# Block-sparse attention and a two-layer FFN on one core: K, Q and V loads moved out of the attention stages, turned heads spread over four PSUM spaces

## The chip, the core and the metric

The kernel runs on one NeuronCore of a Trainium2 chip. The metric is device time in microseconds of one execution; a figure for a kernel is the median of several executions. Engine names are those of the profile: PE multiplies matrices (PEld loads its weights), DVE is VectorE, ACT is ScalarE, POOL is GpSimd, SP is SyncE.

## The reference, cut to what matters

```python
def _attn_ref(q, k, v, sampled_blocks):          # q, k, v: 4 x 8 x 768 x 64
    block, n_blocks = 32, 24
    scores = scale * np.matmul(q, k.transpose(0, 1, 3, 2))
    mask = np.abs(blk_i - blk_j) <= 1
    mask = mask | (blk_i == 0) | (blk_j == 0) | (blk_i == n_blocks - 1) | (blk_j == n_blocks - 1)
    for qb in range(n_blocks):
        for kb in sampled_blocks[qb]:            # 3 sampled key blocks for each query block
            mask[qb * block:(qb + 1) * block, kb * block:(kb + 1) * block] = True
    attn = softmax(np.where(mask, scores, -1e9))
    return np.matmul(attn, v)

def _moe_ref(x, w_in, w_out):                    # x: 3072 x 512, w_in: 512 x 2048, w_out: 2048 x 512
    return (gelu_exact(x @ w_in) @ w_out)
```

The attention output of the four batches, heads side by side, is the x of the FFN.

## The kernel before

**Stages.** Each batch is cut into two halves of 384 tokens, which gives eight units, numbered 0 to 7. Units 0, 2, 4 and 6 are the first halves (they also do the first and last query blocks against all keys, the "dense" rounds), units 1, 3, 5 and 7 the second. The order is written out by hand and each engine runs its own list in that order: attention of unit 0, then for n = 0 to 7 the first FFN product of unit n (FFN1: eight calls of `ffn1_step`, each eight matmuls and one Gelu), and then the attention of unit n+1, with the matmuls of the second FFN product of unit n (FFN2) dealt out between its rounds by a quota. In the main loop (line 515) `fresh` says that unit n+1 begins a new batch: it holds for n = 1, 3 and 5. So a "first half" FFN1 is n = 0, 2, 4, 6 and a "second half" FFN1 is n = 1, 3, 5, 7.

**What a new batch needs.** K and Q of a batch arrive as four DMAs (`load_kq`, two of K into `kn`, two of Q into `qn`), V as eight, one per head (`load_v`, into the V columns of `kvs[b % 2]`). All are issued on POOL. For a new batch each pair of heads of K and Q is turned on PE (`turn_heads`, 16 transposes) into a PSUM tile and placed in SBUF (`place_heads`, K on DVE, Q on ACT); `prep` does the two with the one PSUM tile `psT`. Eight pairs (k0 to k3, q0 to q3) are done, one in each step s = 0 to 7 of the second-half FFN1. When K has been placed, DVE copies the key and value blocks that unit n+1 will read into `gb`: `gather_fixed` (five large copies) and `gather` (33 small copies of K and V columns together, at block numbers held in registers).

**When the loads go out.** `hold_loads(m)` is a copy of one element of `g` on POOL: POOL goes on only when the Gelu of FFN1 column block m is done, so the DMAs behind it wait for that. Four V loads of batch 1 are issued before the first attention; four more wait for step 0 of FFN1(0). K and Q of the next batch wait for the last step of the first-half FFN1 (`hold_loads(14)`), so they run in the attention that follows. The V loads of later batches go out four at a time at step 0 of each FFN1.

**PSUM.** `psA` has two buffers (scores, FFN1), `psV` one (attention output `av`), `psT` one (turned tiles), `psO` one (FFN2 output `op`). During FFN1 `psV` and `psO` hold nothing.

Of the kernel before, what the change touches and what calls it, by code (L numbers as in the profile page):

```python
# [10 lines left out]
BF16 = mybir.dt.bfloat16  # L11
I32 = mybir.dt.int32
AF = mybir.ActivationFunctionType
# [6 lines left out]
def kernel(  # L20
# [11 lines left out]
    P = 128  # L32
    B, H, S, D = q.shape
# [14 lines left out]
    PI = 8  # L48
    PP = S // PI
# [12 lines left out]
    psA = ctx.enter_context(tc.tile_pool(name="psA", bufs=2, space=PSUM))  # L62
    psV = ctx.enter_context(tc.tile_pool(name="psV", bufs=1, space=PSUM))
    psT = ctx.enter_context(tc.tile_pool(name="psT", bufs=1, space=PSUM))
    psO = ctx.enter_context(tc.tile_pool(name="psO", bufs=1, space=PSUM))
# [9 lines left out]
    k0 = qT1.rearrange("p (n c) -> p n c", c=KC)  # L75
# [21 lines left out]
    def keys(b):  # L97
        return k0 if b == 0 else kvs[b % 2][:, :, 0:KC]

    def load_kq(dst, src, b, hs):  # L100
        nc.gpsimd.dma_start(out=dst[0:PP, hs],
                            in_=src[b, hs].rearrange("h (p i) d -> p h (i d)", i=PI))

    def load_v(b, h):
        G, hh = divmod(h, 4)
        c0 = KC + V2 * G + VW * (hh % 2)
        nc.gpsimd.dma_start(out=kvs[b % 2][32 * hh:32 * hh + 32, 0:NB, c0:c0 + D],  # L107
                            in_=v[b, h].rearrange("(n p) d -> p n d", p=BL))
# [13 lines left out]
    def hold_loads(m):  # L122

        nc.gpsimd.tensor_copy(mark, g[0:1, m, 0:1])  # L124

    def ones(i):
        for hh in range(4):
            c0 = KC + VW * (hh % 2) + D
            nc.gpsimd.memset(kvs[i][32 * hh:32 * hh + 32, 0:NB, c0:c0 + V2 + 1:V2], 1.0)
# [46 lines left out]
    def block_numbers(js, engine):  # L176
        flat = vf.rearrange("o j r -> o (j r)")
        vals = []
        for c0 in range(js[0] * NR, (js[-1] + 1) * NR, 22):
            c1 = min(c0 + 22, (js[-1] + 1) * NR)  # L180
            _, got = nc.values_load_multi_w_load_instructions(
                flat[0:1, c0:c1], engines=[engine], min_val=0, max_val=NB,
                skip_runtime_bounds_check_because="block numbers are below the number of blocks")
            vals += got if isinstance(got, (tuple, list)) else [got]
        return {j: vals[NR * i:NR * i + NR] for i, j in enumerate(js)}

    def turn_heads(which, pr, pt):

        src = kn if which == "k" else qn
        for i in range(PI):  # L190
            for h2 in range(2):
                r = h2 ^ (pr // 2)
                nc.tensor.transpose(pt[64 * r:64 * r + 64, i, :],  # L193
                                    src[0:PP, 2 * pr + h2, i * D:(i + 1) * D],
                                    identity[0:PP, 0:PP])

    def place_heads(b, which, pr, pt, on_act):
        if which == "k":
            dst = keys(b)[:, 0:NB, BL * pr:BL * pr + BL].rearrange("q n (a i) -> q n a i", i=PI)
            seen = pt.rearrange("q i (n a) -> q n a i", n=NB)  # L200
            if on_act:
                nc.scalar.copy(dst, seen)
            else:
                nc.vector.tensor_copy(dst, seen)  # L204
        else:
            dst = qTs[b % 2][:, pr, :].rearrange("q (p i) -> q p i", i=PI)
            seen = pt.rearrange("q i p -> q p i")
            if on_act:
                nc.scalar.mul(dst, seen, 1.0 / 8.0)
            else:  # L210
                nc.vector.tensor_scalar_mul(dst, seen, 1.0 / 8.0)

    def prep(b, which, pr, on_act):
        pt = psT.tile([P, PI, PP], BF16, name="pt", tag="T")
        turn_heads(which, pr, pt)
        place_heads(b, which, pr, pt, on_act)

    def spare_key(b):
        kT = keys(b)
        nc.vector.tensor_copy(kT[:, NB, :], kT[:, 0, :])  # L220

    def gather_fixed(b, js, copy):

        kT, n, groups = keys(b), len(js), gb.rearrange("p (g x) -> p g x", x=GW)
        for lane in range(3):
            m = len(range(lane, n, 3))
            c0, j = BW + KC * lane, js[0] + lane - 1
            copy(groups[:, 0:m, c0:c0 + 3 * BW].rearrange("p g (w c) -> p g w c", c=BW)[:, :, :, 0:KC],
                 kT[:, j:j + 3 * m, :].rearrange("p (g w) c -> p g w c", w=3))
        copy(groups[:, :, 0:3 * KC].rearrange("p g (l c) -> p g l c", c=KC),  # L230
             kT[:, None, 0:1, :].to_broadcast([P, NG, 3, KC]))
        copy(groups[:, :, 4 * BW:GW].rearrange("p g (l x) -> p g l x", x=DW)[:, :, :, NR * BW:DW],
             kT[:, None, NB - 1:NB, :].to_broadcast([P, NG, 3, KC]))

    def gather(b, js, at, i0, c0=0, c1=BW, engine=None):

        src = k0 if (b, c1) == (0, KC) else kvs[b % 2][:, :, c0:c1]
        for i, j in enumerate(js, i0):
            for r in range(NR):
                (engine or nc.vector).tensor_copy(sampled(i, r)[:, None, c0:c1],  # L240
                                                  src[:, bass.ds(at[j][r], 1), :])
# [93 lines left out]
    def table(func):  # L335

        nc.scalar.activation(junk, zero[0:1, 0:1], func)  # L337
# [147 lines left out]
    DVE, POOL = mybir.EngineType.DVE, mybir.EngineType.Pool  # L485
    J0, J1 = units[0].js, units[1].js
    value_list()
    known = block_numbers(J0[:7], DVE)
    spaces = [psA.tile([P, 2, 1024], BF16, name="pk", tag="A") for _ in range(2)]
    spaces.append(psV.tile([P, 2, 1024], BF16, name="pq", tag="V"))  # L490
    spaces = [x[:, i, 0:S].rearrange("p (i c) -> p i c", i=PI) for x in spaces for i in range(2)]
    spaces.append(psT.tile([P, PI, PP], BF16, name="pt", tag="T"))
    spaces.append(psO.tile([P, PI, PP], BF16, name="pt", tag="op"))
    for i, (which, pr) in enumerate([(w, pr) for w in "kq" for pr in range(NPR)]):
        turn_heads(which, pr, spaces[i])
        place_heads(0, which, pr, spaces[i], True)
    spare_key(0)
    gather(0, J0[:7], known, 0, 0, KC)
    gather_fixed(0, J0, nc.vector.tensor_copy)
# [4 lines left out]
    others = block_numbers(J0[7:], POOL)  # L504
    gather(0, J0[7:], others, 7, 0, KC, nc.gpsimd)
    gather(0, J0[7:], others, 7, KC, BW, nc.gpsimd)
    ones(1)
    for h in range(4):
        load_v(1, h)
    attention(units[0], iter(()), [0] * 11, (0, 0), 7,  # L510
              {6: [lambda: gather(0, J0[:7], known, 0, KC, BW)]})
    nc.vector.tensor_copy(kvs[0][:, :, 0:KC], k0)
# [2 lines left out]
    for n, unit in enumerate(units):  # L515
        nxt = units[n + 1] if n + 1 < len(units) else None
        b = unit.b
        fresh = nxt is not None and nxt.b != b
        if nxt is not None and not fresh:
            gather_fixed(b, J1, nc.vector.tensor_copy)  # L520
            gather(b, J1[:6], known, 0)
            for i0, i1 in ((6, 9), (9, 11)):
                gather(b, J1[i0:i1], block_numbers(J1[i0:i1], DVE), i0)
        for s in range(KOUT // 2):
            ffn1_step(n, 2 * s)
            if s == 0:
                if not fresh and b + 1 < B:
                    hold_loads(0)
                    for h in range(4, H):
                        load_v(b + 1, h)  # L530
                if fresh and b + 2 < B:
                    hold_loads(0)
                    for h in range(4):
                        load_v(b + 2, h)
                if fresh:
                    others = block_numbers(J0[7:], DVE)
            if s == 7:
                if not fresh and b + 1 < B:
                    hold_loads(14)
                    for hs in HALVES:  # L540
                        load_kq(kn, k, b + 1, hs)
                    for hs in HALVES:
                        load_kq(qn, q, b + 1, hs)
                if nxt is not None:
                    table(AF.Exp)
            if fresh:
                prep(b + 1, "k" if s < 4 else "q", s % 4, s >= 4)
                if s == 3:
                    spare_key(b + 1)
                    gather_fixed(b + 1, J0, nc.vector.tensor_copy)  # L550
                    gather(b + 1, J0[:7], known, 0)
                    gather(b + 1, J0[7:], others, 7)
        filler = ffn2_pieces(n)
        if nxt is None:
            for _ in filler:
                pass
        elif fresh:
            attention(nxt, filler, [4] * 8 + [1, 1, 0], (3, 11))
        else:
            attention(nxt, filler, [6, 5, 5, 5, 5, 6, 2], (3, 11))  # L560
# [30 lines left out]
```

## Time and profile before

| what | value |
|---|---|
| median of 3 runs | 354.41 us (352.02 to 354.45) |
| the profiled execution | 352.95 us, of which the span from first to last instruction is 350.9 us |
| PE busy / weight loads | 277.8 us (79%) / 152.0 us (43%) |
| DVE busy | 220.3 us (63%) |
| ACT busy | 211.7 us (60%) |
| POOL busy | 51.4 us (15%) |
| mean granted clock of PE | 0.951 |
| DMA read and written | 27.26 MB and 6.29 MB |

The table is an average over stages with different limits. The stage is the thing to read: a period is the time from the first matmul of one FFN1 to the first matmul of the next, and holds one FFN1 and one attention. All four first-half periods run the same program on other data, and so do the three second-half periods.

### The profile page before, as it was taken

The page shows a single profiled execution, that of the slowest core. Times are in us where ns is not written, and L with a number is a line of the kernel's source. Part 1 is how long each engine was busy: PE and PEld are TensorE (multiplying, and loading weights), DVE is VectorE, ACT ScalarE, POOL GpSimd, SP SyncE. Part 2 cuts the span into 40 slices and gives each one's busy share as a digit, 9 for nine tenths or more (in the row PEclk, how much of TensorE's full clock was granted, in tenths as well). Part 3 has the DMA queues.
Part 4 walks back from the last instruction along what each step waited for, and adds up shares of the span by engine and source line. Part 5 has one row for each costly group of instructions (what it writes and reads, how often), then busy time and mean ns, then how long its engine had stood idle before and what let it go on. Part 6 is the DMA issues. An engine that isn't in the chain of part 4 may idle for free.

```text
span 350.9 us, 12646 instructions
## 1 busy us (share of the span) xinstructions
PE 277.8 (79%) x5544; PEld 152.0 (43%) x5544; DVE 220.3 (63%) x555; ACT 211.7 (60%) x364; POOL 51.4 (15%) x101
## 2 busy tenths in 40 slices
PE   1732648958798888986898878987898978988994
PEld 1500434533454445543454445543553455445641
DVE  5598619663269898482269897484279878583000
ACT  8555423792358784693358784695358784785521
POOL 8578002310030000330030000330000000000000
PEclk9999856996999999996999999998999999999999
DMA  7999990992190010984190010994000000000001
GB/s 119 129 138 207 187 23 7 43 181 49 47 47 1 32 35 32 47 130 92 57 47 0 32 36 32 47 137 106 35 2 1 34 34 32 3 32 34 32 30 60
DMA packets 39192, 20.72 MB, mean 59 GB/s; under 512 B 25825, under 2 KB 36066, under 8 KB 39138
## 3 DMA queue, kind: packets, MB, share of 16 engines
q0 software_dynamic: 35680, 13.63, 49.8%
q1 hardware_dynamic: 3458, 6.29, 4.9%
q8 instruction: 43, 0.70, 0.9%
q14 instruction: 11, 0.09, 0.1%
HBM read 27.26 MB, written 6.29 MB: 96 GB/s over the span
## 4 chain that ended last, share of the span: by engine, by line
PE 55%; DVE 18%; ACT 18%; issue 7%; DVEq 0%; ACTq 0%
PE hp L418 24%; PE op L426 15%; PE av L373 8%; ACT pp L310 7%; DVE nm L298 4%; PE sc L273 3%; DVE nm L301 3%; DVE gb L240 3%; DVE pT L327 2%; PE pt L193 2%; ACT os L431 2%; ACT L337 2%; DVE xh L390 2%; PE av L349 2%; ACT kv L141 2%
## 5 line engine op out<-in xcount | busy, mean ns | idle before, releaser
L310 ACT ACTIVATE pp<-sc,nm 128x256 bf16<-128x256 f32 (+1 forms) x192 | 91.2, 592 | 19.3 <-DVE nm L298 11.0
L426 PE MATMUL op<-w_out_sb,g 128*128 128x512 bf16 x384 | 99.8, 395 | 3.7 <-ACT os L431 3.7
L418 PE MATMUL hp<-xT,w_in_sb 128*128 128x384 bf16 x512 | 89.4, 330 | 7.0 <-ACT xT L405 7.0
L420 ACT ACTIVATE g<-hp 128x768 bf16<-128x768 f32 x64 | 51.9, 810 | 46.9 <-PE hp L418 46.9
L418 PEld LDWEIGHTS <-w_in_sb 128*128 128x128 bf16 x512 | 48.8, 99 | 39.6 <-issue 9.3
L298 DVE TENSOR_REDUCE nm<-sc 128x4 f32<-128x1024 f32 (+1 forms) x48 | 53.3, 1110 | 16.1 <-PE sc L273 15.9
L426 PEld LDWEIGHTS <-g 128*128 128x128 bf16 x384 | 34.1, 100 | 47.7 <-issue 17.9
L240 DVE COPY gb<-kv 128x388 bf16 (+1 forms) x252 | 46.7, 269 | 7.0 <-issue 6.9
L373 PE MATMUL av<-kv,pT 64*32 64x130 bf16 x1760 | 34.9, 235 | 10.1 <-DVE xh L390 3.7
L373 PEld LDWEIGHTS <-pT 64*32 64x32 bf16 x2816 | 29.7, 96 | 28.3 <-issue 15.5
L431 ACT COPY os<-op 128x512 f32<-128x512 f32 x24 | 14.1, 586 | 40.0 <-PE op L426 40.0
L273 PE MATMUL sc<-gb,qT 64*32 64x256 bf16 x704 | 20.4, 289 | 22.0 <-ACT pp L310 12.9
L327 DVE STREAM_TRANSPOSE pT<-pp 128x512 f32<-128x512 f32 (+1 forms) x48 | 31.6, 657 | 6.7 <-ACT pp L310 6.7
L273 PEld LDWEIGHTS <-qT 64*32 64x32 bf16 x832 | 11.0, 90 | 54.0 <-issue 42.6
L373 PE MATMUL av<-gb,pT 64*32 64x130 bf16 x1056 | 21.9, 235 | 9.5 <-issue 9.4
L386 DVE TENSOR_SCALAR den<-av 128x8 f32<-128x8 f32 (+2 forms) x28 | 4.5, 160 | 38.4 <-PE av L373 36.2
L124 POOL COPY mark<-g 1x1 bf16<-1x1 bf16 x8 | 2.7, 338 | 169.8 <-ACT g L420 169.8
L405 ACT COPY xT<-tx 128x512 bf16<-128x512 bf16 (+1 forms) x24 | 13.5, 561 | 22.0 <-PE tx L400 22.0
L204 DVE COPY kv<-pt 128x768 bf16<-128x768 bf16 x12 | 11.5, 958 | 21.8 <-PE pt L193 21.8
L107 POOL DMA_DIRECT2D kv<-in_v_dram x32 | 23.1, 730 | 2.2 <-DMA qn<-in_q_dram 1.3
L337 ACT ACT_TABLE_LOAD x15 | 19.2, 1283 | 0.3
L390 DVE TENSOR_TENSOR xh<-av,rec 128x512 bf16<-128x512 f32 (+2 forms) x28 | 18.3, 652 | 1.0
(56 smaller groups left out, 195.1 us busy)
## 6 DMA issues: line engine op xcount, KB each, us to landing
out_dram<-os SPq DMA_DIRECT2D x24, 256.0 KB, 2.0
kn<-in_k_dram POOLq DMA_DIRECT2D x8, 384.0 KB, 5.7
qn<-in_q_dram POOLq DMA_DIRECT2D x8, 384.0 KB, 8.6
kv<-in_v_dram POOLq DMA_DIRECT2D x32, 96.0 KB, 5.7
w_in_sb<-in_moe_w_in_dram POOLq DMA_DIRECT2D x4, 512.0 KB, 12.5
w_out_sb<-in_moe_w_out_dram POOLq DMA_DIRECT2D x2, 1024.0 KB, 20.8
raw<-in_sampled_blocks_dram SPq DMA_DIRECT2D x1, 0.6 KB
```

The source lines that it names most:

```text
L107: nc.gpsimd.dma_start(out=kvs[b % 2][32 * hh:32 * hh + 32, 0:NB, c0:c0 + D], in_=v[b, h].rearrange("(n p) d -> p n d", p=BL))
L240: (engine or nc.vector).tensor_copy(sampled(i, r)[:, None, c0:c1], src[:, bass.ds(at[j][r], 1), :])
L273: nc.tensor.matmul(o, lhsT=qT[rows, pr, BL * j:BL * j + BL], rhs=rhs(rows, pr), start=True, stop=True)
L298: nc.vector.tensor_reduce(out=nm[:, 0:2 * n].rearrange("p (g j) -> p g j", g=2), in_=A4[:, :, 0:n, :], op=ALU.max, axis=AX.X, negate=True)
L310: nc.scalar.activation(dst.rearrange("p (c k e) -> p c e k", e=2, k=BL), src.rearrange("p (c e k) -> p c e k", e=2, k=BL), AF.Exp, bias=bias)
L327: nc.vector.transpose(pt[:, 0:w].bitcast(F32), pp[:, 0:w].bitcast(F32))
L337: nc.scalar.activation(junk, zero[0:1, 0:1], func)
L373: nc.tensor.matmul(av[32 * s:32 * s + 32, h, V2 * G:V2 * G + V2], lhsT=pv[rows, c // 2, :, c % 2], rhs=src[rows], start=(c == 0), stop=(c ...
L390: nc.vector.tensor_tensor(xh[rows, :, 0:m * D].rearrange("p h (x d) -> p h x d", d=D), a[:, :, :, 0:D], rec[rows, :, 0:m, None].to_broadca ...
L418: nc.tensor.matmul(hp[:, i, 0:T], lhsT=w_in_sb[:, ki, (m + i) * P:(m + i + 1) * P], rhs=xTs[n % 2][:, ki, 0:T], start=(ki == 0), stop=(ki ...
L420: nc.scalar.activation(g[:, m:m + 2, 0:T], hp[:, :, 0:T], AF.Gelu)
L426: nc.tensor.matmul(op, lhsT=g[:, m, t * P:(t + 1) * P], rhs=w_out_sb[:, m, :], start=(m == 0), stop=(m == KOUT - 1))
```

## The change

K and Q of the next batch are issued at step 0 of the first-half FFN1, behind `hold_loads(0)`, and no longer behind `hold_loads(14)`. All eight V loads of a batch are issued at step 0 of a second-half FFN1; for batch 1 four of them go out in FFN1(0), behind K and Q, and four in FFN1(1), ahead of the eight of batch 2. No load is issued before the first attention any more except those for batch 0 and the weights.

`prep` is gone. `spaces()` hands out four PSUM spaces: `psT`, the two banks of `psV` and `psO`. k0 and k1 are turned in step 0, k2 and k3 in step 1, q0 to q3 in steps 2 to 5; the gathers come after step 1 and no longer after step 3. The start of the kernel takes its last four spaces from `spaces()` too, in another order.

```diff
-    def prep(b, which, pr, on_act):
-        pt = psT.tile([P, PI, PP], BF16, name="pt", tag="T")
-        turn_heads(which, pr, pt)
-        place_heads(b, which, pr, pt, on_act)
+    def spaces():
+
+        views = [psT.tile([P, PI, PP], BF16, name="pt", tag="T")]
+        two = psV.tile([P, 2, 1024], BF16, name="pq", tag="V")
+        views += [two[:, i, 0:S].rearrange("p (i c) -> p i c", i=PI) for i in range(2)]
+        return views + [psO.tile([P, PI, PP], BF16, name="pt", tag="op")]
...
     ones(1)
-    for h in range(4):
-        load_v(1, h)
     attention(units[0], iter(()), [0] * 11, (0, 0), 7,
...
             if s == 0:
                 if not fresh and b + 1 < B:
                     hold_loads(0)
-                    for h in range(4, H):
-                        load_v(b + 1, h)
-                if fresh and b + 2 < B:
-                    hold_loads(0)
-                    for h in range(4):
-                        load_v(b + 2, h)
-                if fresh:
-                    others = block_numbers(J0[7:], DVE)
-            if s == 7:
-                if not fresh and b + 1 < B:
-                    hold_loads(14)
                     for hs in HALVES:
                         load_kq(kn, k, b + 1, hs)
                     for hs in HALVES:
                         load_kq(qn, q, b + 1, hs)
-                if nxt is not None:
-                    table(AF.Exp)
+                    if b == 0:
+                        for h in range(4):
+                            load_v(1, h)
+                if fresh and (b == 0 or b + 2 < B):
+                    hold_loads(0)
+                    if b == 0:
+                        for h in range(4, H):
+                            load_v(1, h)
+                    if b + 2 < B:
+                        for h in range(H):
+                            load_v(b + 2, h)
+                if fresh:
+                    others = block_numbers(J0[7:], DVE)
+            if s == 7 and nxt is not None:
+                table(AF.Exp)
             if fresh:
-                prep(b + 1, "k" if s < 4 else "q", s % 4, s >= 4)
-                if s == 3:
+                if s in (0, 2):
+                    views = spaces()
+                for which, pr in {0: ("k0", "k1"), 1: ("k2", "k3"), 2: ("q0",), 3: ("q1",), 4: ("q2",),
+                                  5: ("q3",)}.get(s, ()):
+                    pr = int(pr)
+                    turn_heads(which, pr, views[pr])
+                    place_heads(b + 1, which, pr, views[pr], which == "q")
+                if s == 1:
                     spare_key(b + 1)
                     gather_fixed(b + 1, J0, nc.vector.tensor_copy)
                     gather(b + 1, J0[:7], known, 0)
```

## Rows read from the trace of the kernel before

**Rows 1.** Chain that ended last, whole span: start us, length us, what.

```profile
43.33 4.56 issue
...
55.67 11.88 PE hp L418 x64
...
76.82 3.41 issue
...
137.30 10.57 PE hp L418 x64
...
158.65 3.29 issue
...
239.57 2.07 issue
```

**Rows 2.** Busy time by period: stretch, length, engines (instructions), clock, DMA share, GB/s.

```profile
core 0: us, PE busy (x) PEld busy (x) DVE busy (x) ACT busy (x) POOL busy (x), PEclk, DMA share, GB/s
55.67:94.89 39.22, 32.38 (x564) 16.53 (x564) 23.07 (x60) 21.50 (x40) 6.21 (x10) 0.88 0.56 66
94.89:137.30 42.41, 37.31 (x823) 20.35 (x822) 34.43 (x80) 29.20 (x50) 3.00 (x5) 1.00 0.29 30
137.30:173.76 36.46, 30.76 (x564) 16.60 (x564) 19.71 (x55) 21.49 (x40) 6.46 (x10) 0.91 0.65 78
...
216.40:250.54 34.14, 29.77 (x565) 16.06 (x564) 19.61 (x55) 21.51 (x40) 6.46 (x10) 0.95 0.69 83
250.54:293.08 42.54, 37.41 (x822) 20.26 (x822) 34.49 (x80) 29.21 (x50) 0.00 (x0) 1.00 0.06 22
293.08:324.16 31.08, 28.35 (x565) 15.51 (x564) 19.06 (x55) 21.50 (x40) 0.00 (x0) 1.00 0.08 28
```

**Rows 3.** The same view in two microseconds of attention 1.

```profile
78.00:80.00 2.00, 0.00 (x0) 0.00 (x0) 0.00 (x0) 1.01 (x3) 0.00 (x0) 0.71 1.12 236
```

**Rows 4.** DMA queues of the page: packets, MB, share of 16 engines.

```profile
q8 instruction: 43, 0.70, 0.9%
```

**Rows 5.** Busy time and PE instructions, counted from the start of a q8 packet.

```profile
60.32:77.90 17.58, 15.09 (x262) 7.93 (x260) 13.04 (x34) 14.08 (x28) 5.18 (x9) 1.00 1.05 98
...
60.32:74.22 13.90, 12.86 (x127) 6.37 (x126) 10.39 (x32) 10.77 (x20) 5.18 (x9) 1.00 1.02 73
144.19:155.87 11.68, 10.26 (x123) 4.66 (x128) 7.27 (x13) 10.02 (x20) 2.84 (x5) 1.00 0.93 76
```

**Rows 6.** DMA queues from 62 to 77.8 us (q0, q1; no q8).

```profile
q0 software_dynamic: 3718, 1.56, 106.7%
```

**Rows 7.** DMA queues from 77.8 to 79 us.

```profile
q8 instruction: 1, 0.02, 5.1%
```

**Rows 8.** Timeline of POOL: start us, length us, line, operation, count, idle before.

```profile
69.06 1.34 POOL L101 DMA_DIRECT2D kn<-in_k_dram  x2 [0.37 <-issue]
...
97.96 2.82 POOL L107 DMA_DIRECT2D kv<-in_v_dram  x4 [0.40 <-DVE kv L204]
...
140.44 2.91 POOL L107 DMA_DIRECT2D kv<-in_v_dram  x4
```

**Rows 9.** Busy time and DMA in stretches of load traffic (columns of Rows 2).

```profile
99.50:103.90 4.40, 4.40 (x58) 2.48 (x58) 2.55 (x5) 1.66 (x3) 1.28 (x2) 1.00 2.19 92
...
70.80:80.30 9.50, 4.67 (x183) 2.64 (x186) 5.48 (x7) 7.68 (x19) 0.92 (x2) 0.92 1.10 191
...
41.50:46.50 5.00, 0.92 (x39) 0.46 (x37) 1.59 (x4) 2.04 (x6) 0.00 (x0) 0.50 3.33 98
```

**Rows 10.** Timeline of the end of FFN1(3) and the start of attention 4.

```profile
181.32 0.96 DVE L204 COPY kv<-pt 128x768 bf16<-128x768 bf16 x1 [0.91 <-PE pt L193]
...
185.22 5.70 DVE L240 COPY gb<-kv 128x388 bf16 x33
...
188.22 0.53 PE L193 MATMUL pt<-identity,qn 96*64 96x96 bf16 x16
...
189.21 1.28 ACT L337 ACT_TABLE_LOAD   x1
...
191.82 2.28 ACT L310 ACTIVATE pp<-sc,nm 128x768 bf16<-128x768 f32 x2 [0.42 <-DVE nm L301]
```

More of the change, by code (lines that the diff above doesn't have):

```diff
@@ L488 @@
     known = block_numbers(J0[:7], DVE)
[L489 to L493, printed above, removed]
+    first = [psA.tile([P, 2, 1024], BF16, name="pk", tag="A") for _ in range(2)]
+    first = [x[:, i, 0:S].rearrange("p (i c) -> p i c", i=PI) for x in first for i in range(2)]
+    first += spaces()
     for i, (which, pr) in enumerate([(w, pr) for w in "kq" for pr in range(NPR)]):
-        turn_heads(which, pr, spaces[i])
-        place_heads(0, which, pr, spaces[i], True)
+        turn_heads(which, pr, first[i])
+        place_heads(0, which, pr, first[i], True)
     spare_key(0)
```

## The prediction

> **What bounds the kernel now.** I read the chain that ended last first, then cut the span into periods, and only then looked at the queues. The chain is mostly PE, and in it stand four long pieces called "issue": time in which PE waited for nothing that the profile shows, 4.56 us in attention 0 and 3.41, 3.29 and 2.07 us in attentions 1, 3 and 5 [rows 1]. The periods say what these pieces cost in all. The four first-half periods have the same PE work, 564 or 565 matmuls, and should be equal; they take 39.22, 36.46, 34.14 and 31.08 us [rows 2]. The last is the only one in which no K, Q or V is loaded (POOL is empty in it), and the only one with the clock at 1.00 throughout; the others were granted 0.88, 0.91 and 0.95. The second-half periods, three of them, take 42.41 to 42.64 us at full clock, whether POOL issues four V loads in them or none [rows 2].
>
> Next, what the stop is. In the middle of the one in attention 1, PE, weight loads and DVE do nothing, DMA moves 236 GB/s, and the granted clock falls to its lower level, 1.2 GHz, within the row (0.71 over two microseconds) [rows 3]. The queue called instruction moved 43 packets [rows 4]; PE ran 5,544 matmuls and as many weight loads, 11,088 in all, so one packet is some 258 PE instructions. From the start of one such packet at 60.32 to 77.90 us PE began 262 matmuls and 260 weight loads, two packets' worth, and stood still [rows 5]. The first of these two was used up at 74.22 (127 and 126 instructions) [rows 5], so a new packet was due from then; but up to 77.8 the queue shows none, while the K and Q packets ran [rows 6], and it came only after [rows 7]. I read this as: PE holds two blocks of instructions, asks for another when one is used, and the answer stood behind the K and Q traffic for some 3.6 us, which is longer than the remaining block lasts in the dense part of an attention.
>
> **The change part by part.** The sum is made against the profiled execution: 352.95 us, a span of 350.86 and 2.1 around it. The median of the runs is 1.46 above it.
>
> *K and Q out of attentions 1, 3 and 5.* What they cost there is the excess of the three periods over the one without loads: 8.14, 5.38 and 3.06 us. In the first, FFN1(0) itself ran 1.31 us longer (11.88 against 10.57 [rows 1]) because the clock was still low from attention 0; I leave that in, which makes 6.83. Sum 15.27 us. It holds the stops and what follows from them (the slow clock after each).
>
> Do the loads now stop PE elsewhere? In FFN1(2), POOL, held by the same mark, issues its loads from 140.44, 3.1 us after the first matmul at 137.30 [rows 1, 8]. K and Q take four issues of 0.67 us; in attention 1 their traffic began 1.7 us after the first issue and lasted to 80.3, 9.5 us at 191 GB/s with an output store among it [rows 8, 9]; without that an estimate is 8 us (1.56 MB [rows 6] at that rate). So they run from about 4.9 to 12.9 us after the first matmul, and FFN1 lasts 10.6: they still reach 2.3 us into the attention. A fetch that falls due in that time is late by some 3.6 us, as above. But FFN1 uses few instructions: after the fetch at 144.19, in FFN1(2), the next 256 lasted 11.68 us, and after the one at 60.32 13.90 us [rows 5]. A delay of 4 us, even of the whole 8, is covered. If that cover were gone, each period would pay its stop again, 3 to 7 us. The two marks of `hold_loads(14)` and the wait behind them cost nothing now and their going gives nothing.
>
> *V out of attention 0.* Here the weights' traffic goes over into the four V loads of batch 1, whose traffic fills 41.5 to 46.5 us, DMA share 3.33, clock 0.50, PE nearly idle [rows 9], and the stop is 4.56 us [rows 1]. The weights remain, so not all must go. Lower bound: a stop of the longest kind seen with other traffic stays (3.41), gain 1.15. Upper bound: stop gone and the clock back for FFN1(0), 4.56 + 1.31 = 5.87. The clock had fallen before the V traffic began, so I take the middle, 3.5.
>
> *V in other places.* Four V loads take 4.4 us of traffic [rows 9]. FFN1(0) now has K, Q and four V, to about 17.4 us after its first matmul; FFN1(1) has twelve V, about 13 us of traffic, to 17.7; FFN1(3) eight. In attention 1 the next fetch falls due 13.9 us after that at 60.32, 18.5 us after the first matmul of FFN1(0); the traffic ends a microsecond earlier. So I count nothing, with up to 6.8 (the whole excess of that period) as the other end. The second-half periods carry four V loads without a trace of cost.
>
> *The new wait.* The gather after step 1 of FFN1(1) copies V columns of batch 1, whose last four loads are issued only in that FFN1. DVE stands behind it with all of attention 2's maxima. The V loads issue from 97.96 in this FFN1 and their traffic is over at 103.9, 9 us after its first matmul at 94.89 [rows 8, 9]. The gather couldn't start earlier anyway: an FFN1 step with its transposes is 1.87 us (eight from 173.76 to 188.75) and 16 transposes are 0.5 [rows 2, 10], so k2 is turned 4.2 us after the first matmul, and with two placements of 0.96 after each other k3 is placed at 6.2; from there to the gather now pass 2.9 us (182.28 to 185.22 [rows 10]). So 9.1 against 9.0: nothing, within a microsecond either way.
>
> *Turned heads earlier.* PE does the same 128 transposes and eight steps, so FFN1 is no shorter. What ends last in it now: the gather ends at 190.92 [rows 10], the last Gelu is followed by the table load at 189.21, and q3 is placed on ACT behind that; the first exponentials start at 191.82 [rows 10]. After the change DVE is done about 15 us after the first matmul (k3 at 6.2, then 8.6 us of copies, as from 182.28 to 190.92 now), as FFN1 ends and before the first maximum can be taken, and q3 is long placed. But the last Gelu comes some 0.5 us later, because the transposes that followed the last matmuls (0.53 at 188.22 [rows 10]) then stand ahead of them: the table load would end at 191.0, and a 0.2 us first use of it at 191.2. The late one is then the table load, and the gain 0.6 us for each of units 4 and 6, and between 0 and 0.6 for unit 2. I take 1.5 in all; bounds -1 (the copies beside POOL's issues lengthen and DVE is late again) and 2.5.
>
> Sum: 15.27 + 3.5 + 1.5 = 20.3 us. 352.95 - 20.3 = 332.7; on the scale of the median, 334.
>
> **Two rules of the Trainium skill that speak against this.** The row shows a fetch 3.6 us late behind K and Q [rows 5 to 7]. "DMA: Bandwidth & Descriptors", section "Queues, rings and completion order", says that each DMA engine serves the rows of its queues in turn, packet by packet. By that rule a fetch in a row of its own would not stand behind the loads, the stops would have another cause, and moving loads would give little; that is the third rival below. Row and rule can be reconciled only if each turn is slow; the trace shows the delay. The other: POOL's four V issues in FFN1(1) took 2.82 us while DVE placed k1, after a wait of 0.40 put down to DVE [rows 8]. "SBUF — State Buffer", section "A bandwidth-pool intuition that's wrong (but worth ruling out)", says that certain DVE copies keep POOL from writing the descriptors of its DMAs. Were that so for the whole of the DVE work in FFN1(1), it would give the second rival.
>
> **The rivals.** First, *the tail*: V traffic behind K and Q in FFN1(0), or the twelve V loads, outlast FFN1, a fetch in attention 1 is late after all, and the period keeps its excess: 334 + 6.8 = 341. For it: only a microsecond of room. Against: after the request at 74.22 PE went on to 76.82 [rows 1, 5], so 2.6 us of delay more are free. 12%.
>
> Second, *the gather's wait*: in FFN1(1) DVE's copies hold POOL back until `gather_fixed` is done at 9.1 us; then 2.1 to the last of four issues and 3.8 to the end of its traffic (100.1 to 103.9 [rows 8, 9]), 5.7 of gather and 0.96 of maximum: 21.7 us, where the first exponentials now start at 18.06 (191.82 less 173.76). Price 3.6, and the 0.3 of that unit is lost: 338. Against: the issues beside k1 weren't slowed. 5%.
>
> Third, *not the loads*: the stops stay where they are for another reason and only the earlier gather counts: 352.9. Against: the period without loads has none. 4%.
>
> Fourth, *slower*: the late fetch goes with the traffic into FFN1. It decides from the point where a fetch is held for longer than a block lasts there, 11.7 to 13.9 us [rows 5]. Price: the 15.27 come back there, and V, now two and three times as much at once, stops FFN1(1) and (3) as it did attention 0, 4.56 and 1.31 of slow clock each, 11.7. That is 27.0 against the gain of 20.3, so 354.4 + 6.7 = 361. Against: the V loads that are in those halves now don't lengthen them (10.57 in FFN1(2) [rows 1], 42.41 and 42.54 with and without [rows 2]). 4%.
>
> **How the numbers follow.** Forecast 75%: 334, its own range 330 (attention 0 at its upper bound, the earlier gather at 2.5: 3.4 more) to 339 (attention 0 at its lower bound and the gather at -1: 4.9 less). The range that should hold the time 8 times in 10 is 330 to 343: the forecast's own and the first two rivals, with two microseconds of room. One per cent is about what a measurement of this kernel can tell from no change (its three runs differ by 0.7%). Faster by over 1%: 75 + 12 + 5 = 92%; within 1%: 4%; slower: 4%.
>
> **What would show it.** Right: the three first-half periods with loads come to 31 to 32 us, but for 1.3 more in the first, at a clock near 1.00; no "issue" piece over 1.5 us in attentions 1, 3 and 5; instruction packets at their usual distance there; the stop in attention 0 under 3.4 us; the first exponentials of units 4 and 6 0.6 us earlier after the FFN1's start. Wrong: an "issue" piece in an FFN1, or at the start of attention 1 or 2; the gather of FFN1(1) ended after 17 us, with a DMA named as what it waited for; the second-half periods over 43 us. What would make the prediction wrong is that the delay of a fetch is not some 4 us but as long as the traffic, or that PE's stock in FFN1 is smaller than the counts say.

## The result, and the profile after

The changed kernel takes 337.62 us (median; 336.57 to 338.6) against 354.42, a ratio of 0.9541 with a 95% interval of 0.9492 to 0.9591. The forecast was 334, its range 330 to 343: the direction and most of the size hold. Of the gain, 3.6 us are missing by the medians. The profiled execution took 337.74 us, with a span of 335.93, so 14.93 us went from the span, where the prediction's terms sum to 20.3; by the profiles 5.4 are missing.

The start and the seven periods, busy time by stretch as in [rows 2] (same columns):

```profile
0.00:51.81 51.81, 23.05 (x711) 15.48 (x712) 35.20 (x94) 29.78 (x43) 23.49 (x57) 0.90 1.45 129
51.81:85.66 33.85, 29.75 (x560) 16.10 (x565) 23.31 (x60) 21.50 (x40) 5.88 (x9) 0.95 0.76 76
85.66:130.63 44.97, 37.54 (x816) 20.65 (x822) 35.07 (x80) 29.06 (x50) 9.09 (x13) 0.96 1.35 46
130.63:163.64 33.01, 28.14 (x559) 15.63 (x564) 19.50 (x55) 21.49 (x40) 3.38 (x5) 1.00 0.38 74
163.64:205.11 41.47, 35.95 (x817) 20.35 (x822) 34.83 (x80) 28.95 (x50) 6.10 (x9) 1.00 0.88 41
205.11:236.33 31.22, 27.69 (x560) 15.51 (x565) 19.38 (x55) 21.51 (x40) 3.38 (x5) 1.00 0.40 78
236.33:277.88 41.55, 35.92 (x816) 20.24 (x822) 34.28 (x80) 28.94 (x50) 0.00 (x0) 1.00 0.06 22
277.88:309.22 31.34, 27.90 (x559) 15.54 (x564) 19.06 (x55) 21.50 (x40) 0.00 (x0) 1.00 0.08 27
```

Behind the start, call them period 0 to 6, after the FFN1 each begins with. Against before:

| stretch | us gained | forecast |
|---|---|---|
| start | 3.86 | 3.5 |
| period 0 | 5.37 | 6.83 |
| period 1 | -2.56 | 0.3 |
| period 2 | 3.45 | 5.38 |
| period 3 | 1.17 | 0.6 |
| period 4 | 2.92 | 3.06 |
| period 5 | 0.99 | 0.6 |
| period 6 | -0.26 | 0 |

Three of them miss: 0, 2 and, by most, 1, the only period that became clearly longer.

The chain that ended last (start, length, what), with the pieces in attention 0, 1 and 3 and the one new piece (the second line from the same view of 45 to 90 us alone):

```profile
43.04 1.00 issue
...
73.20 0.40 issue
...
80.73 0.88 issue
...
90.43 6.92 DMA kv<-in_v_dram
...
151.98 1.18 issue
```

The 4.56 us of attention 0 are 1.00. In attention 1 and 3 pieces of 0.40 and 1.18 us, 21.4 us after the first matmul of FFN1(0) and of FFN1(2), are left of 3.41 and 3.29, which stood at 21.2 and 21.4. The 0.88 in attention 1 is no rest of the long stop: it was there before, as

```profile
89.87 0.97 issue
```

What is new is a DMA on the chain: the last of the V loads that the gather of FFN1(1) needs, from its issue to its landing. The timeline there (start, length, line, operation, count, idle time before):

```profile
97.67 5.92 DVE L242 COPY gb<-kv 128x388 bf16 x33 [2.26 <-DMA kv<-in_v_dram]
...
103.51 1.81 DVE L303 TENSOR_REDUCE nm<-sc 128x1 f32<-128x768 f32 x2
...
102.31 1.04 PE L428 MATMUL op<-w_out_sb,g 128*128 128x512 bf16 x4
105.65 0.51 PE L275 MATMUL sc<-kv,qT 64*32 64x512 bf16 x8 [2.30 <-ACT pp L312]
106.08 1.83 PE L428 MATMUL op<-w_out_sb,g 128*128 128x512 bf16 x4
```

Busy time of PE in the same place (length, busy, granted clock, DMA share, GB/s):

```profile
103.35:105.65 2.30, 0.00 (x1) 1.00 0.65 12
105.65:107.65 2.00, 2.00 (x12) 0.63 0.03 8
107.65:109.65 2.00, 2.00 (x12) 0.51 0.00 0
```

DVE waits 2.26 us for V and starts the 33 copies 12.0 us after the first matmul of FFN1(1), not 9.1 as forecast. The first maximum (the first step of the softmax) is late and PE stands still for 2.30 us. Behind that the granted clock is at its lower level for some 4 us (0.63 and 0.51): four FFN2 matmuls take 1.83 us, where the four ahead of the pause take 1.04.

### The profile page after: what moved, and what is told of

Its sections match the earlier page's. It is cut to its first block, busy times and chain, and to the rows that moved or that the text cites. A ratio compares the mean times of both kernels' runs of the same rounds, so it can differ in the third digit from the quotient of the medians.

```text
span 335.9 us, 12597 instructions
## 1 busy us (share of the span) xinstructions
PE 267.1 (80%) x5505; PEld 150.4 (45%) x5544; DVE 220.6 (66%) x555; ACT 211.0 (63%) x364; POOL 51.3 (15%) x98
## 4 chain that ended last, share of the span: by engine, by line
PE 53%; ACT 20%; DVE 18%; issue 5%; DMA 2%; POOL 1%; DVEq 0%; ACTq 0%
PE hp L420 22%; PE op L428 14%; ACT pp L312 9%; PE av L375 7%; DVE nm L300 5%; PE sc L275 3%; DVE gb L242 3%; DVE pT L329 3%; ACT os L433 2%; ACT L339 2%; PE av L351 2%; DVE xh L392 2%; DMA kv<-in_v_dram 2%; DVE nm L303 2%; ACT g L422 2%
## 5 line engine op out<-in xcount | busy, mean ns | idle before, releaser
L428 PE MATMUL op<-w_out_sb,g 128*128 128x512 bf16 x345 | 89.1, 384 | 7.3 <-ACT os L433 3.7
L242 DVE COPY gb<-kv 128x388 bf16 (+1 forms) x252 | 46.0, 258 | 8.8 <-issue 6.4
L375 PE MATMUL av<-kv,pT 64*32 64x130 bf16 x1760 | 33.7, 229 | 9.7 <-DVE xh L392 4.1
L375 PEld LDWEIGHTS <-pT 64*32 64x32 bf16 x2816 | 28.7, 93 | 20.7 <-DVE xh L392 8.6
L275 PE MATMUL sc<-gb,qT 64*32 64x256 bf16 x704 | 20.3, 289 | 19.0 <-ACT pp L312 12.9
L375 PE MATMUL av<-gb,pT 64*32 64x130 bf16 x1056 | 21.4, 230 | 3.0 <-issue 3.0
L303 DVE TENSOR_REDUCE nm<-sc 128x1 f32<-128x768 f32 x16 | 15.1, 951 | 2.8 <-PE sc L275 2.8
```

Of the source, the lines that this page charges most:

```text
L275: nc.tensor.matmul(o, lhsT=qT[rows, pr, BL * j:BL * j + BL], rhs=rhs(rows, pr), start=True, stop=True)
L375: nc.tensor.matmul(av[32 * s:32 * s + 32, h, V2 * G:V2 * G + V2], lhsT=pv[rows, c // 2, :, c % 2], rhs=src[rows], start=(c == 0), stop=(c ...
L428: nc.tensor.matmul(op, lhsT=g[:, m, t * P:(t + 1) * P], rhs=w_out_sb[:, m, :], start=(m == 0), stop=(m == KOUT - 1))
```

## The experiments

All of them start from the changed kernel. Its own program, profiled twice, gave 33.85 and 35.20 us for period 0 and within 0.6 us for the others. The spread is wider than that: in the profiles below, periods 5 and 6 run from 41.36 to 42.95 and from 31.04 to 31.91 us where no edit touches them, and FFN1(0) alone from 11.9 to 13.3. The first eight experiments were executed once each, on two chips on which the kernel before took 356.69 and 350.76 us. So they are read by their periods and stops, with these spreads in mind, and their totals only roughly.

**K and Q back behind the last Gelu.**

```diff
-                if not fresh and b + 1 < B:
+                if not fresh and b == 0:
                     hold_loads(0)
-                    for hs in HALVES:
-                        load_kq(kn, k, b + 1, hs)
...
+            if s == 7 and not fresh and b + 1 < B:
+                hold_loads(14)
+                for hs in HALVES:
+                    load_kq(kn, k, b + 1, hs)
...
```

> K and Q of the next batch go back behind the last Gelu of the first-half FFN1; all else is as in the changed kernel (V loads, turned heads). Late fetch (my theory): the stops return in attentions 1, 3 and 5, each with no instruction packet between the start of the K and Q traffic and the stop; the three first-half periods go from 33.9, 33.0 and 31.2 us back to some 38, 36.5 and 34, so the execution is 10 to 12 us longer, 348 to 350. Rival, the gain came from the earlier heads and the later V loads and K and Q count for nothing: periods stay, 337 to 338.

It took 352.88 us, more than the 348 to 350 that I had expected. The chain:

```profile
73.41 4.60 issue
...
159.34 3.31 issue
...
239.19 1.77 issue
```

All three stops are back, and the queue of the instruction packets shows none from 58 us until 75.7, after the first stop has begun. Periods 0, 2 and 4 are 41.38, 36.49 and 33.52 us for 33.85, 33.01 and 31.22 in the changed kernel: 7.53 + 3.48 + 2.30 = 13.3. Of the first, 0.75 is FFN1(0) itself (12.87 us for 12.12), which is within its spread. The rest of the 15 lies in periods 5 and 6 (1.4 and 0.6), which no K and Q reach, so it is not put down to them. K and Q carry most of the gain.

**K and Q in the middle.** The same with `s == 4` and `hold_loads(8)`.

> K and Q wait for the Gelu of step 4 of the first-half FFN1, so that most of their traffic, about 10 to 18 us after its first matmul, lies in the attention, but ends before the fetch that falls due 18.5 us after it. Late fetch: a fetch that is late is harmless while the block before it lasts, so the periods stay within 1 us of the changed kernel (33.9, 33.0, 31.2) and the execution at 337 to 340. Rival, load traffic in an attention costs by its length: about three quarters of what the late loads cost comes back, 8 us in all, 345 to 347.

It took 339.86 us. Periods 0, 2 and 4:

```profile
51.78:86.28 34.50, 29.61 (x559) 16.07 (x564) 23.10 (x60) 21.54 (x40) 6.22 (x10) 0.96 0.64 75
...
132.32:164.59 32.27, 28.14 (x560) 15.62 (x565) 19.06 (x55) 21.53 (x40) 2.98 (x5) 1.00 0.40 76
...
206.76:237.96 31.20, 27.69 (x559) 15.49 (x564) 18.95 (x55) 21.53 (x40) 2.97 (x5) 1.00 0.40 78
```

Most of the traffic is now in the attention (in period 2 it runs from 9.6 to 18.4 us after the first matmul, and FFN1 lasts 10.6) and costs nothing that stands out of the spread (+0.65, -0.74, -0.02). With the run before, this says that load traffic in an attention doesn't stop PE as such; traffic does at the moment when a block of instructions falls due and the one before it is used up fast.

**No loads.** The K, Q and V loads of batches 1 to 3 are left out altogether.

> Leaves out the K, Q and V loads of batches 1 to 3 altogether (the kernel goes on with batch 0's K and Q and what lies in the V columns). Late fetch and place of the block ends: attention 1 and 3 keep short stops of PE, because a block ends there just ahead of the dense matmuls, and FFN1(0) its slow clock: first-half periods 0 and 2 stay near 33.5 and 32.8 us, 4 and 6 near 31.2; only period 1 falls, from 45.0 to 41.6, for its gather waits for no load. 334 us. Rival, the rest of the excess of periods 0 and 2 is the tail of the moved traffic: they fall to 32.5 and 31.3, 331 us.

It took 335.37 us. Periods 0 to 2, then the chain:

```profile
51.54:85.97 34.43, 30.17 (x560) 16.21 (x564) 22.03 (x60) 21.52 (x40) 0.00 (x0) 0.94 0.05 18
85.97:127.34 41.37, 35.64 (x817) 20.23 (x822) 34.30 (x80) 28.93 (x50) 0.00 (x0) 1.00 0.06 22
127.34:160.27 32.93, 28.16 (x560) 15.62 (x565) 19.06 (x55) 21.50 (x40) 0.00 (x0) 1.00 0.08 27
```

```profile
148.70 1.37 issue
```

With nothing to load at all, periods 0 and 2 stay where they are, with the stop in attention 3. So what is left there is no tail of the moved traffic; the first rival, the tail, falls. Period 1 drops by 3.6 us: its loss is the loads'.

The stop in attention 3 can be read as in [rows 5], from an instruction packet that began at 133.45 us; then the instruction queue from 147.25 to 148.7:

```profile
133.45:145.90 12.45, 10.82 (x123) 5.12 (x129) 7.26 (x13) 10.30 (x21) 0.00 (x0) 1.00 0.06 21
133.45:148.70 15.25, 13.46 (x264) 6.88 (x264) 9.99 (x18) 12.73 (x27) 0.00 (x0) 1.00 0.05 19
```

```profile
q8 instruction: 1, 0.02, 4.9%
```

The first block is used up at about 145.9, and the next packet begins at 147.29: 1.4 us later, with none of the loads running. Behind K and Q, before the change, it was 3.7 (74.22 to 77.91). PE goes on at 150.07, some 4.2 us after the block was used up, and the second block had lasted only 2.8. By this reading the short stops are the fetch's own time, wherever a block is used up faster than that; the loads lengthen it.

**168 PE instructions more.** Behind the turned heads of batch 0:

```diff
+    idle = psT.tile([P, PI, PP], BF16, name="idle", tag="T")
+    for i in range(84):
+        nc.tensor.transpose(idle[0:PP, i % PI, :], identity[0:PP, 0:PP], identity[0:PP, 0:PP])
```

> 84 transposes of the identity, with their weight loads 168 PE instructions, are added after the turned heads of batch 0, where PE is idle; they shift the ends of PE's instruction blocks by 168 against the program, nothing else. From period to period these ends now move later by some 40; 168 earlier is 88 later, so by the theory of the block ends periods 0 and 2 should stand as 4 and 6 do now: the piece of 0.9 in attention 1 and the ones of 1.2 and 0.7 in attention 3 go, period 2 falls from 33.0 to 31.4; periods 4 and 6 get places not seen yet, up to 2 us longer. Rival, the pieces belong to their place in the program or to the loads: periods 0, 2, 4 and 6 stay within 0.4 us of 33.9, 33.0, 31.2 and 31.3.

It took 341.98 us; FFN1(0) starts 2.6 us later, the price of the transposes. Periods 2 and 3, and the chain:

```profile
132.81:164.05 31.24, 27.89 (x559) 15.55 (x564) 17.66 (x45) 21.50 (x40) 2.84 (x5) 1.00 0.41 78
164.05:208.28 44.23, 37.22 (x817) 20.71 (x823) 37.67 (x97) 28.95 (x50) 6.10 (x9) 0.96 0.83 38
```

```profile
201.77 1.34 issue
```

Period 2 is down by 1.77 us to 31.24, as expected, and its pieces of 1.18 and 0.73 are gone (one of 0.41 is new); in attention 1 the 0.40 is gone and the 0.88 is 0.49. Period 0 didn't follow: 33.34, with an FFN1(0) of 12.85 us. A stop of 1.34 us turns up in attention 4, which had none above 0.2, with a fall of the clock behind it, and period 3 is 2.76 longer. Behind the start, nothing but the place of the block ends was moved. So the small stops move with the blocks. How much of the 2.76 is the stop's is less sure: the last run below has a period 3 of 43.96 us with no block moved.

**Turned heads back.** One PSUM space, one pair in each step, the gathers after step 3; the loads stay.

```diff
-                for which, pr in {0: ("k0", "k1"), 1: ("k2", "k3"), 2: ("q0",), ...
...
+                pt = psT.tile([P, PI, PP], BF16, name="pt", tag="T")
+                turn_heads("k" if s < 4 else "q", s % 4, pt)
+                place_heads(b + 1, "k" if s < 4 else "q", s % 4, pt, s >= 4)
-                if s == 1:
+                if s == 3:
```

> Turned heads as before (one PSUM space, k0 to k3 in steps 0 to 3, q0 to q3 in steps 4 to 7, gathers after step 3); the loads as in the changed kernel. If the heads are worth what the profile shows, periods 3 and 5 lengthen by 1.0 each (41.5 to 42.5). Period 1: if its loss is the gather's wait for the last four V loads of batch 1, which landed 11.7 us after the first matmul, the gather gets there only then (about 11.5) and the period stays at 45 or grows by no more than 0.7. Rival, its loss is from the heads in the other PSUM spaces or from DVE and POOL in each other's way in the first steps: period 1 falls back to 42.5. 339.5 us by the first, 337 by the rival.

It took 339.16 us. Periods 1 and 3, then DVE in FFN1(1) and PE behind it:

```profile
87.02:130.36 43.34, 36.78 (x816) 20.44 (x822) 35.03 (x80) 29.06 (x50) 8.62 (x13) 1.00 1.38 48
...
162.55:205.47 42.92, 36.71 (x816) 20.36 (x822) 34.62 (x80) 29.08 (x50) 5.81 (x9) 1.00 0.84 39
```

```profile
98.93 5.88 DVE L242 COPY gb<-kv 128x388 bf16 x33
...
104.73 1.81 DVE L303 TENSOR_REDUCE nm<-sc 128x1 f32<-128x768 f32 x2
...
106.87 0.50 PE L275 MATMUL sc<-kv,qT 64*32 64x512 bf16 x8 [0.75 <-ACT pp L312]
107.31 1.04 PE L428 MATMUL op<-w_out_sb,g 128*128 128x512 bf16 x4
```

Periods 3 and 5 lengthen by 1.45 and 1.07, but period 5 stays within its spread. Surer is the time from the first matmul of FFN1(3) and FFN1(5) to the first exponentials: 17.15 to 17.22 us in every profile with the earlier heads, 18.33 and 18.06 here, 18.06 before the change. The earlier heads are worth 0.9 to 1.2 us each time. Period 1 was called wrongly by both sides, 43.34 against 45 and 42.5. The gather begins 11.9 us and the first maximum 17.7 us after the first matmul, hardly sooner than in the changed kernel (12.0 and 17.85). But here ACT still has q3 to place, PE's idle time falls into two parts of 0.92 and 0.75 us, and its matmuls go on at full speed. From the eight score matmuls behind the pause to the start of the third group of FFN2 matmuls after them, the same work takes 3.55 us here (106.87 to 110.42) and 5.14 in the changed kernel (105.65 to 110.79). That is 1.6 us, the size of the difference between the two periods.

**The loads behind V out of the way.** The eight V loads of batch 2 wait for the Gelu of step 4 of FFN1(1) (`if s == 4 and fresh and b == 0: hold_loads(8)`).

> The eight V loads of batch 2 wait for the Gelu of step 4 of FFN1(1), behind the four of batch 1 that the gather needs; all else is as in the changed kernel. If the gather of FFN1(1) is late because the loads behind its four share the DMA engines, the four land 9 to 9.5 us after the first matmul instead of 11.7, the gather ends near 15.5, PE has no idle time of 2.3 us before attention 2 and the clock stays up: period 1 falls from 45.0 to 41.8 to 42.5, the execution to 334.5. Rival, POOL's issues or DVE's own copies make the four land late: nothing changes, 337.5.

It took 340.33 us, and period 1 is 46.59, not better (it was 46.04 in the second run above, where no edit touches it). POOL in FFN1(1) and the chain there, then DVE, then a stretch of the traffic (columns of [rows 2]):

```profile
89.13 2.81 POOL L107 DMA_DIRECT2D kv<-in_v_dram  x4
...
91.23 6.36 DMA kv<-in_v_dram
...
97.84 5.84 POOL L107 DMA_DIRECT2D kv<-in_v_dram  x8 [0.38 <-issue]
```

```profile
97.91 7.53 DVE L242 COPY gb<-kv 128x388 bf16 x33 [2.21 <-DMA kv<-in_v_dram]
```

```profile
94.00:96.00 2.00, 2.00 (x27) 1.14 (x25) 1.63 (x3) 1.63 (x3) 0.00 (x0) 1.00 0.98 15
96.00:98.00 2.00, 2.00 (x26) 1.10 (x24) 0.09 (x1) 1.51 (x2) 0.34 (x2) 1.00 0.00 0
```

My expectation was wrong. With nothing behind them the last of the four V loads still lands at 97.6, 11.1 us after the first matmul, and the gather starts at 11.5, though the packets are through by 96 us. What was to be avoided is not the queue behind but the plain time from issue to landing. And the eight issues now lie beside the gather, whose 33 copies take 7.53 us for 5.92.

**V of batch 1 as before.** Four loads ahead of attention 0, four in FFN1(0) behind K and Q, none in FFN1(1).

> V of batch 1 as before the change: four loads ahead of attention 0, four in FFN1(0) behind K and Q, none in FFN1(1), which keeps the eight of batch 2. Late fetch: the stop of some 4.5 us returns in attention 0 and FFN1(0) starts 3.5 to 4 us later; the gather of FFN1(1) waits for no load and period 1 falls to 41.5 to 42.2. The two are about equal: 338 to 339. Rival, the stop in attention 0 came from the weights alone and was shortened by chance: FFN1(0) starts within 1 us of 51.8, and the execution is 335.

It took 339.31 us. The stop of attention 0 is 4.29 us again and FFN1(0) starts at 55.16, 3.35 later; period 1 is 41.46. Both halves came close to what was expected:

```profile
43.10 4.29 issue
```

**All V of batch 1 in FFN1(0).** All eight behind K and Q, none in FFN1(1).

> All eight V loads of batch 1 in FFN1(0) behind K and Q, so that the gather of FFN1(1) waits for none; the eight of batch 2 stay in FFN1(1). Period 1 falls to 41.5 to 42.2. The traffic from FFN1(0) now lasts to some 20 us after its first matmul (16 to 17 in the changed kernel), over the fetch that falls due at 19.0. If a fetch is late behind V traffic as it is behind K and Q, attention 1 gets a stop of 2 to 4 us and period 0 rises from 33.9 to 37 or more: 337 to 338. If V traffic delays a fetch by little, period 0 stays and the execution is 334.5.

It took 341.48 us, where I had expected 337 to 338: period 1 falls to 41.97, and period 0 rises to 40.88, with the old stop:

```profile
73.28 4.69 issue
```

So four more V loads behind K and Q delay the fetch as K and Q do in an attention: its packet comes at 74.42 us, 22.9 after the first matmul. In the changed kernel the loads' traffic ends at 71.5, 19.7 us after the first matmul, and the packet begins at 71.24; without any load it begins just as late (19.7). So the changed kernel stands close to this edge.

**V of batch 1 issued earlier, and the changed kernel again.**

```diff
+        if fresh and b == 0:                     # ahead of step 0 of FFN1(1)
+            nc.gpsimd.tensor_copy(mark, xTs[n % 2][0:1, 0, 2 * P:2 * P + 1])
+            for h in range(4, H):
+                load_v(1, h)
...
```

> V of batch 1, heads 4 to 7, no longer waits for the first Gelu of FFN1(1) but for the last copy into its xT, so POOL issues it at the first matmul and not 2.7 us after it; the eight loads of batch 2 stay behind the Gelu. If the time from issue to landing (6.4 to 6.9 us after the last of the four issues) is what makes the gather late, the four land 9 us after the first matmul, the gather starts at once behind its fixed part, PE has no idle time of 2.3 us, and period 1 falls from 45.0 to 41.5 to 42.3: the execution 2.5 to 3.3 us under the changed kernel of the same call, ratio to it 0.991. Rival, the landing hangs on something else in FFN1 (DVE's placements, the eight loads behind): period 1 stays within 0.7 us of 45.

> The changed kernel again, for a comparison on one chip: 0.954 of the kernel before, 337 to 339 us, periods within 0.7 us of 33.9, 45.0, 33.0, 41.5, 31.2, 41.6 and 31.3.

It took 334.65 us (median of seven, 333.31 to 335.33; ratio to before 0.9476, 0.9425 to 0.9527) beside 338.78 for the changed kernel on the same chip (median of six, 337.45 to 339.16; 0.9582, 0.9529 to 0.9635): 0.988 of it by the medians, and the two ranges don't meet. POOL, DVE and period 1:

```profile
85.67 2.82 POOL L107 DMA_DIRECT2D kv<-in_v_dram  x4 [0.31 <-issue]
```

```profile
94.88 5.93 DVE L242 COPY gb<-kv 128x388 bf16 x33 [0.21 <-DMA kv<-in_v_dram]
```

```profile
85.10:126.58 41.48, 36.48 (x822) 20.32 (x822) 34.85 (x80) 28.98 (x50) 9.12 (x14) 1.00 1.48 50
```

The first issue moved from 2.67 to 0.57 us after the first matmul, the wait shrank from 2.26 to 0.21 us, the pause of PE is gone, and period 1 falls by 3.49. The late landing is the cause of its loss: the loss goes when the loads come earlier, by this edit or by the old order two runs above. The version beats both kernels.

**Half of w_out later as well.** `load_w_out(1)` waits for the last copy into `xTs[0]` and goes out at the first matmul of FFN1(0), ahead of K, Q and V.

> The early V loads of the run above, and the second half of w_out is loaded only at the first matmul of FFN1(0), ahead of K, Q and V. If the remaining stops of attention 0 (1.2 and 1.0 us) and the slow clock of FFN1(0) come from the weights' traffic, the stops go, FFN1(0) starts 2 to 4 us earlier and lasts 10.6 us and not 12.1, and the execution is 3.5 to 5 us under the run above. The price: the traffic of FFN1(0) is 5 us longer, to some 18 to 19 us after its first matmul, where the next fetch falls due; if it is late, attention 1 has a stop of 3 to 4 us and period 0 rises to 38, and the gain is lost. Rival, the clock of attention 0 is low from its waits between engines alone: FFN1(0) starts within 1 us of 51.8 and stays at 12 us.

It took 335.19 us (331.62 to 338.74), ratio to before 0.9449 (0.938 to 0.9517): no difference from the run above that can be told. The profile is of the longest of its six executions, 338.74 us, so its sizes may not hold for the others. In it FFN1(0) starts 1.6 us earlier than in the run above, at 49.92, and attention 1 pays:

```profile
71.90 2.44 issue
```

The two pieces of attention 0 are 0.30 and 0.45 us, for 1.22 and 1.00 in the changed kernel; FFN1(0) is still slow (12.71). The weights are a part of what is left in attention 0, as far as one profile shows it; the slow clock there isn't explained by their second half. Attention 4, which this edit doesn't touch, has a stop of 0.69 us and then a clock of 0.50, and period 3 is 43.96 us.

## Why the prediction was right, and where a term was mis-sized

**K and Q.** Right in kind: the stops went when the traffic was moved, came back when it was moved back, and stayed away when it overlapped an attention but no fetch that was urgent. "A delay of 4 us, even of the whole 8, is covered" held: no stop in any FFN1. The size was forecast as 15.27 and came as 11.74 in the three periods. The part that failed is taking period 6 as what the others would be without loads. They run the same instructions, but blocks of 256 end at other places in each; without any load, periods 0 and 2 are 34.43 and 32.93 us. The prediction also put the whole "3.6 us" of the late fetch down to K and Q; 1.4 of it passes without any load, by the run without loads. FFN1(0) also kept its slow clock (12.12 us), as left in by the sum. Two of the signs named for being right so failed: periods 0 and 2 did not come to 33.3 and 32 us or less.

**Attention 0.** 3.5 forecast, 3.86 measured, 3.35 when undone. The 3.5 was the middle between bounds of 1.15 and 5.87, so that it came so near is partly luck.

**The new wait.** This is the step that was mis-sized: "So 9.1 against 9.0: nothing". I took the end of the traffic for the landing. The trace of before would have told: the page gives 5.7 us from issue to landing, and a last issue at 100.1 with that is 10.9 us after the first matmul, not 9.0. Measured: 11.5 to 12.0, a gather 2.4 to 2.9 late, and behind it a pause of PE with the clock low after it, which no term had. Together 2.56 us lost where 0.3 was to be gained. Three signs that I had named for being wrong came here: the gather ended 17.9 us after the first matmul, a DMA is named as what it waited for, and the period is over 43 us. The second rival had the place, and its price of 3.6 + 0.3 stands against 2.86 measured, but it didn't have the mechanism: DVE did not hold POOL back. Ten issues beside its copies took 0.74 us each, against 0.71 before. That its total of 338 is the measured one is chance, for part of what is missing lies in K and Q. The Trainium skill says in "SBUF — State Buffer", section "A bandwidth-pool intuition that's wrong (but worth ruling out)", that such copies can keep POOL from writing descriptors; no run here shows that, and the delayed engine was DVE (7.53 us for 5.92).

**Turned heads.** 0.6 forecast for each of periods 3 and 5, 1.17 and 0.99 measured by the periods. The step is as described: the last Gelu's table load now ends last, with the first exponentials right behind it (ACT, start of attention 4):

```profile
179.39 1.28 ACT L339 ACT_TABLE_LOAD   x1
...
180.79 2.04 ACT L312 ACTIVATE pp<-sc,nm 128x768 bf16<-128x768 f32 x2
```

They start 17.15 us after the first matmul, for 18.06 before: 0.9 and not 0.6.

**The rivals.** The tail did not show in the changed kernel, but there was no room left: its traffic in FFN1(0) lasted 19.7 us after the first matmul, where 17.4 was forecast, and four more V loads bring the tail, at 7.0 us in period 0 (40.88 for 33.85), near the price of 6.8 that I gave it. "Not the loads" is refuted by the first experiment, "slower" by the result. "DMA: Bandwidth & Descriptors" in the Trainium skill, section "Queues, rings and completion order", has each DMA engine serve its queues in turn; the fetch is late behind K and Q and behind V all the same. Why, these runs don't tell: in none was the traffic's form changed alone, and that stays open.

## What to carry to other kernels

Look for time in which PE waits for nothing, and set it beside the instruction packets and the load traffic: a transfer that is off every data path can still stop an engine with many small instructions. Put bulk loads where the instruction rate is low, and count a load from its issue to its landing, not to its last packet, when something waits for it. Before taking one stage as the control for another, ask what differs between them besides the thing in question.

## What the runs showed that I had not expected

- PE stops for up to some 1.4 us at the end of a block of instructions without any load traffic, depending on where it ends: 1.37 us in attention 3 with no loads. A stop of 1.34 us turned up in attention 4 after a shift by 168 instructions. The closest that two instruction packets begin in any of the profiles is 3.29 us; whether that is a floor, no run tests. The Trainium skill, "Runtime: NRT & Kernel Launch", section "Instruction fetch mechanics", gives 256 instructions to a block, which the trace bears out, and calls the crossing mostly hidden, which the dense attention stages here do not bear out.
- A pause of PE of 2.30 us was followed by 1.6 us of loss in slower matmuls, at a granted clock of 0.63 and 0.51. In attention 4 of the last run the clock went to 0.50 behind a stop of 0.69 us, and with the heads back it kept up behind 0.92 and 0.75. What decides it, these runs don't tell.
- The four V loads with nothing behind them landed about 1.6 us after their traffic had ended (96 us against 97.6).
- The granted clock isn't always recorded. With the heads back, the profile shows 1.00 while FFN1(0) begins at half speed; matmuls of FFN1 (PE busy, PEld busy, granted clock, DMA share, GB/s), first with the heads back, then in the changed kernel:

```profile
51.50:53.50 2.00, 1.95 (x7) 0.94 (x7) 1.00 0.00 0
```

```profile
51.80:53.80 2.00, 1.99 (x7) 0.98 (x7) 0.50 0.00 0
```

Seven matmuls in two microseconds in both; the record of one shows it and that of the other doesn't. So the full clock that I read in period 1 with the heads back rests on its matmuls (four FFN2 matmuls in 1.04 us there), not on the column.
